# Attention followed by a gated product: one buffer for both banks of a block product's accumulator, a third held back, and new due times

## The chip, the cores and the metric

One core of one Trainium2 chip runs the whole program. The metric is device time in microseconds; the kernel before took 578.11 us (median of 3 runs, 578.06 to 578.78).

The names of the engines in the profile: PE is TensorE (matmuls; PEld are its weight loads), DVE is VectorE, ACT is ScalarE, POOL is GpSimd, SP is SyncE, which only issues DMAs here.

## The reference

```python
def _attn_ref(q, k, v):                     # q, k, v: 8 batches x 12 heads x 448 x 64
    S = q.shape[2]
    scores = scale * np.matmul(q, k.transpose(0, 1, 3, 2)) - np.log(S)
    attn = 1.0 / (1.0 + np.exp(-scores))    # a sigmoid, no row sums
    return np.matmul(attn, v)

def _moe_ref(x, w_val, conv_w, w_out):      # x: 8 x 448 x 768, the heads side by side
    for k in range(5):                      # causal convolution of 5 taps, each channel alone
        gate_pre += conv_w[k] * xp[:, k:k + S, :]
    gate = 1.0 / (1.0 + np.exp(-gate_pre))
    val = x @ w_val                         # 768 x 768
    return gate * val @ w_out               # 768 x 768
```

## The kernel before

**Layout and stages.** Channels lie on the 128 partitions, tokens run along the free dimension. Attention works on 48 pairs of heads (i) that go by twos (j, 24 of them; three j make a batch). The work of one j on PE is a chain: `scores_rest` of the next j, `attend` of this j, then `scores` of the next pair (L547, L570, L633, L641). ACT takes the sigmoid and splits the result into a high and a low 16-bit part, DVE takes the low part. Batch 0 is not multiplied on its own: each of the other seven batches carries a seventh of it, so that a product has 512 columns (448 + 64) and batches run from 1 to 7.

For a batch b there follow: the scale of x (`x_largest`, PE at L733), the split of x into two 16-bit parts (`x_split`), the gate (taps on ACT and DVE, some added up by DMAs that POOL issues, L714), the first product "val" (`product`, 6 columns m of 18 matmuls of 512 tokens, L965), the multiplication of its result by the gate on DVE (L975), and the second product "out".

**The block product.** For batches 6 and 7 the second product isn't six columns but `product_mixed`: a 2 x 2 block scheme with seven block products instead of eight. `form` makes from the gated result the seven input blocks (three in a first part of the tiles `form`/`form_hi`, `form_lo`, four in a second part, after sums on DVE at L844), `mix` has made the mixed weights once. The product is done by thirds q (NQ = 3, two column blocks each). A third has seven steps k; a step is nine matmuls of 256 columns (L904; three groups of three, one per c) into one of two banks, and then one evacuation of that bank into `y` with a scale: on ACT or DVE for steps 0, 1, 2 and 6 (L915, which shows as L386 on ACT or L388 on DVE), on DVE alone for steps 3, 4 and 5, which add to `y` (L917). The banks of the seven steps are 0, 1, 0, 1, 0, 1, 0. Steps 0, 3 and 5 use weights of `w_out`, the others the tile `mixed`. Batch 6 writes its results from `y`, batch 7, the last one ("final"), from `y_mixed`.

**Accumulators.** A third's two banks are one tile from the ring `ps_a` (L340: three buffers of two banks each). The same ring serves attention's scores and outputs and, for batch 7, the scale of x at L733. A ring hands out its buffers in the order of the program text, and a buffer's first writer may not be ordered ahead of the first writer of the buffer before it. So the three thirds of batch 6 come after L733 of batch 7, and the three final thirds replace those of batch 6, one by one. The val columns use two other banks (`ps_m0`, `ps_m1`) in turn.

**What sets the order.** The program text only makes a list of operations (`Plan.op`), each with the engines it may run on and their estimated costs, a due time (`prio`), and dependencies that follow from the `Buf` objects it reads and writes. `Plan.issue` (L196) then plays a list scheduler: whenever an engine is free it takes, among the operations that are ready by the estimates, the one with the smallest due time. The resulting order is the order of instructions on each engine. The semaphores between engines are not made from the `Buf` objects, but afterwards from the tiles that the instructions touch. `Buf.part` (L119) makes a second `Buf` for the same tile; operations on the part and on the whole are then independent for the scheduler.

Due times come from `line(i)` (L396: `first` for each of the first 12 pairs, `step` for each later one), `tau(i)` = line(i) + t_i, `turn(b)` = line(6(b + 1)) + b_b, and constants of the table `AT` (L85) for each kind of operation. A val column m is due at turn(b) + product + val_b + m step / 2; step k of third q of batch 6's block product at turn(6) + product + out6 + 3 step + mixed_mid + (q + k / 7) step; of the final one at turn(7) + product + out7 + 3 step + mixed + (3k + q) step / 21. HELD (L64) is how many of the three thirds of batch 6's product are put behind val of batch 7 in the program text (L1103 and L1109); these also get `AT["held"]` added to their due times.

Of the kernel before, what the change touches and what calls it, by code (L numbers as in the profile page):

```python
# [60 lines left out]
OUT_TOP = 13  # L61
HT = T // 2
NQ = NC // 2
HELD = 2  # L64
FORMS = 6
MIXED_FROM = 6
MIX_AT = 13
# [15 lines left out]


AT = dict(  # L85
    first=-23.17, step=19.9, val=118.94, val_step=-180.69, out=170.01, out_step=-585.1, w_max=-224.22,
    w_split=49, load_qk_first=12.5, load_qk=-153.59, load_v=35.43, split_hi=192.57, split_lo=97.07,
    rest_first=-5.45, rest=250.79, a_first=-823.33, a=-1541.85, attend=-104.6, v_max=-108.74, v_exp=-145.56,
    v_split=417.62, x=-65.05, x_max=32.83, x_scale=-888.7, x_hi=232.99, x_lo=156.41, x_step=393.39, tap=-573.02,
    scores=173.83, a_rest=-160.23, a_rest_first=-66.81, tap_first=75.93, tap_pair=-94.59, tap_step=190.04,  # L90
    gate=38.36, product=-249.46, y=72.69, g_hi=-142.47, g_lo=154.31, o=172.23, share=0.47, w_load=-45.48,
    mix=831.29, mix_step=13.64, form=7.6, mixed=12.32, t0=170.5, t1=-311.68, t2=-210.97, t3=24.02, t4=-165.77,
    t5=182.87, t6=37.77, t7=210.54, t8=130.07, t9=-208.47, t10=-178.97, t11=21.32, t12=26.04, t13=159.94,
    t14=143.46, t15=-16.02, t16=-1206.94, t17=269.84, t18=35.94, t19=51.33, t20=-168.57, t21=-153.86,
    t22=-150.38, t23=54.53, t24=-9.1, t25=-119.78, t26=128.3, t27=-16.04, t28=-248.21, t29=-216.39, t30=-23.16,
    t31=-188.65, t32=-25.47, t33=201.84, t34=-112.66, t35=116.16, t36=68.12, t37=132.66, t38=-271.95,
    t39=-148.99, t40=-170.95, t41=-163.89, t42=-172.96, t43=148.71, t44=-73.9, t45=-55.24, t46=-128.06,
    t47=205.12, t48=162.48, t49=-179.83, b0=-52.12, b1=184.23, b2=26.45, b3=-121.12, b4=-98.53, b5=-102.96,
    b6=239.3, b7=117.68, val0=-168.38, val1=-927.67, val2=243.52, val3=-124.5, val4=-183.24, val5=-32.09,
    val6=172.16, val7=-67.59, out0=13.17, out1=32.57, out2=-15.69, out3=-147.76, out4=351.75, out5=161.64,  # L100
    out6=125.89, out7=211.13, form_mid=-11.03, mixed_mid=-129.61, held=-17.53, o_mid=14.69,
)


# [169 lines left out]
def attention_then_gate(  # L274
# [32 lines left out]
    def ring(pool, n, shape, dtype, name):  # L307
        rings.append(Ring(pool, n, shape, dtype, name))
        return rings[-1]
# [8 lines left out]
    v_exp = ring(sb, 3, [P, 4], I32, "v_exp")  # L318
# [14 lines left out]
    x_max = ring(sb, 2, [P, NP], F32, "x_max")  # L333
# [13 lines left out]
    def fixed(shape, dtype, name):  # L347
        t = const.tile(shape, dtype, name=name)
        return Buf(lambda: t)
# [16 lines left out]
    def columns_of(t):  # L366
        return [Buf(t) for _ in range(NC)]
# [3 lines left out]
    w_max = {n: columns_of(fixed([P, NC], BF16, f"{n}_max")) for n in ("val", "out")}  # L371
# [6 lines left out]
    def copy(eng, to, x):  # L378
        if eng == "A":
            nc.scalar.copy(to, x)  # L380
        else:
            nc.vector.tensor_copy(to, x)  # L382
# [7 lines left out]
    def sub(eng, to, x, y):  # L390
        engines[eng].tensor_tensor(to, x, y, op=ALU.subtract)  # L391


    FIRST, STEP = AT["first"], AT["step"]

    def line(i):  # L396
        return min(i, AHEAD) * FIRST + max(i - AHEAD, 0) * STEP
# [4 lines left out]
    def turn(b):  # L402
        return line((b + 1) * NP) + AT[f"b{b}"]
# [368 lines left out]
    mixed = {}  # L772
# [75 lines left out]
    def product_mixed(b, only=range(NQ), late=0.0):  # L848

        final = b == B - 1  # L850
        t = turn(b) + AT["product"] + AT[f"out{b}"] + NC * STEP / 2 + AT["mixed" if final else "mixed_mid"] + late
# [11 lines left out]
        acc, ys, whole_y = {}, {}, {}  # L863

        def begin(q):
            if final:
                x = ps_a.new()
                acc[q] = [(x.part() if n else x, lambda n=n: x()[:, n, :HT]) for n in range(2)]
                y = x_ring.new(lambda: sb.tile([P, 2, T], F32, name="y_mixed", tag="x", bufs=x_ring.n))
                whole_y[q] = y  # L870
                ys[q] = [([y.part(), y.part() if n else y], lambda n=n: y()[:, n, :]) for n in range(2)]
            else:
                if b < IN_A_FROM:
                    x = next(bank)
                    xs = [x.new(), banks[x is banks[0]].new()]
                    acc[q] = [(x, lambda x=x: x()[:, :HT]) for x in xs]
                else:
                    x = ps_a.new()
                    acc[q] = [(x.part() if n else x, lambda n=n: x()[:, n, :HT]) for n in range(2)]
                ys[q] = {}  # L880

        def slot(q, n):
# [53 lines left out]
        if final:  # L936
            for q in range(NQ):
                begin(q)
            for k in range(len(steps)):
                for q in range(NQ):  # L940
                    step(k, q, t + (3 * k + q) * STEP / 21)
        else:
            for q in only:
                begin(q)
                for k in range(len(steps)):
                    step(k, q, t + (q + k / 7) * STEP)

    gv = {}

    def product(n, b, m, late=0.0):  # L950
        t = turn(b) + AT["product"] + AT[f"{n}{b}"] + (m + NC * (n == "out")) * STEP / 2 + late
        h, l = w_hi[n, m], w_lo[n, m]

        def columns(cs, t):
            po = next(bank).new()
            for c in range(NC):
                s = two[3 * b + c // 2]
                if n == "val":
                    x, reads = (lambda k, xs=s["xs"], p=c % 2: xs()[:, k, p * T : (p + 1) * T]), s["xs_in"]
                else:  # L960
                    x, reads = (lambda k, g=gv[b, c]: g()[:, k, :]), [gv[b, c]]

                def emit(e, c=c, x=x):
                    for j, (w, k) in enumerate(((h, 0), (h, 1), (l, 0))):
                        mm(po()[:, cs], w()[:, c, :], x(k)[:, cs], start=(c == 0 and j == 0),  # L965
                           stop=(c == NC - 1 and j == 2))

                op({"P": 0.65 * (cs.stop - cs.start) / T}, t + c * STEP / 12, emit, [*reads, h, l], [po])
            return po

        po = columns(slice(0, T), t)
        t += STEP / 2
        if n == "val" and b >= MIXED_FROM:
            g = st[b * NP + m]["g"]
            op({"V": 0.66}, t + AT["y"], lambda e: nc.vector.scalar_tensor_tensor(  # L975
                g()[:, m % 2, :], po(), y_scale()[:, m : m + 1], g()[:, m % 2, :], op0=ALU.mult, op1=ALU.mult), [po, y_scale], [g], port="")
            if m % 2:
                form(b, m // 2)
            return
        y = y_ring.new()  # L980
        if n == "val":
            g, gate = form_ring.new(lambda: sb.tile([P, 2, T], F16, name="g", tag="form", bufs=FORMS)), st[b * NP + m]["g"]
            gv[b, m] = g

            op({"V": 0.66}, t + AT["y"], lambda e: nc.vector.scalar_tensor_tensor(
                y(), po(), y_scale()[:, m : m + 1], gate()[:, m % 2, :], op0=ALU.mult, op1=ALU.mult), [po, gate, y_scale], [y], port="")
            op({"V": 0.33, "A": 0.53}, t + AT["g_hi"], lambda e: copy(e, g()[:, 0, :], y()), [y], [g])
            op({"G": 1.17, "V": 0.6}, t + AT["g_lo"], lambda e: sub(e, g()[:, 1, :], y(), g()[:, 0, :]), [y], [g])
        else:
            n = (b - 1) * SL  # L990
            op({"A": 0.65, "V": 0.66}, t + AT["o"], lambda e: scaled(
                e, y(), po(), outer[b]()[:, m : m + 1]), [po, outer[b]], [y], port="")
            op({"S": 0.45}, t + 1, lambda e: nc.sync.dma_start(out[b, m], y()[:, :S]), [y], [], P * S * 4)
            op({"S": 0.45}, t + 1.1, lambda e: nc.sync.dma_start(out[0, m, :, n : n + SL], y()[:, S:]), [y], [], P * 1000)
# [52 lines left out]
    for j in range(TWOS):  # L1047
# [7 lines left out]
        if j == 0:  # L1055
            first, attended = attend(j)
            last = attended.then = rest(j + 1)
        else:
            o = rest(j + 1) if j + 1 < TWOS else None
            first, last = attend(j)  # L1060
            if o:
                o.then = first
                o.deps |= {d for d in first.deps if d is not o}
                first = o
# [19 lines left out]
        b = j // 3  # L1084
# [15 lines left out]
        if b > 1:  # L1100
            x_unscale(b)
            if b - 1 >= MIXED_FROM:
                product_mixed(b - 1, range(NQ - HELD) if b == B - 1 else range(NQ))  # L1103
            else:
                for m in range(NC):
                    product("out", b - 1, m)
        for m in range(NC):
            product("val", b, m)
    product_mixed(B - 2, range(NQ - HELD, NQ), AT["held"])  # L1109
    product_mixed(B - 1)  # L1110
    plan.close(rings)
    for o in plan.issue():
# [50 lines left out]
```

## Time and profile before

| | |
|---|---|
| median of 3 runs | 578.11 us (578.06 to 578.78) |
| the profiled execution's own time | 578.0 us |
| span of the profile, first to last instruction | 576.2 us |
| granted TensorE clock | 1.000 |
| PE busy | 566.0 us, 98% of the span |
| DVE busy | 453.5 us, 79% |
| ACT busy | 448.5 us, 78% |
| POOL busy | 155.2 us, 27% |

In a line of the timeline the first two numbers are the start and the length in us, followed by engine, line and operation, what is written and read, and in brackets the idle time before it with what ended it. In the chain of waits each line is a start, a length and the work, "x18" being 18 instructions. In a table by stage each engine has its busy time and, in brackets, its instructions. Matmuls overlap: one of 256 columns is listed with 0.27 us, but the next one starts well before its end.

### The profile page before, as it was taken

How to read it: one execution, taken by the hardware profiler on the slowest of the kernel's cores; microseconds unless marked ns; L12 is line 12 of the kernel's file. 1: busy time of each engine (PE TensorE's matmuls, PEld its weight loads, DVE VectorE, ACT ScalarE, POOL GpSimd, SP SyncE). 2: the span in 40 equal slices, each digit the busy share in tenths (PEclk: the TensorE clock that was granted, in tenths of full speed). 3: DMA queues.
4: the chain of work that ended last, by engine and by line, in shares of the span. 5: the costliest groups of instructions: out<-in, count | busy, mean ns of one | idle time of the engine just before them, and what ended most of it. 6: DMA issues, size and time to landing. Idle time of an engine off the chain costs nothing.

```text
span 576.2 us, 9839 instructions
## 1 busy us (share of the span) xinstructions
PE 566.0 (98%) x3742; PEld 294.1 (51%) x3742; DVE 453.5 (79%) x742; ACT 448.5 (78%) x612; POOL 155.2 (27%) x177
## 2 busy tenths in 40 slices
PE   9999989999999999999999999999999999999897
PEld 5333334455555555545555454554545555545776
DVE  1778999998898988878587886879777889987312
ACT  5777998889998879878798878889688899852231
POOL 0000124344425332252322423223241433110100
PEclk9999999999999999999999999999999999999999
DMA  8798687757584475834667364674636653441213
GB/s 338 283 350 267 182 258 145 191 132 180 129 199 102 115 169 142 214 75 134 127 189 189 77 163 96 171 167 140 169 69 174 157 133 75 95 89 38 73 38 111
DMA packets 39935, 88.45 MB, mean 154 GB/s; under 512 B 14928, under 2 KB 21072, under 8 KB 39888
## 3 DMA queue, kind: packets, MB, share of 16 engines
q0 software_dynamic: 8640, 31.46, 29.5%
q1 hardware_dynamic: 31248, 56.37, 29.4%
q8 instruction: 29, 0.48, 0.3%
q14 instruction: 18, 0.15, 0.1%
HBM read 43.96 MB, written 12.40 MB: 98 GB/s over the span
## 4 chain that ended last, share of the span: by engine, by line
PE 94%; ACT 4%; DVE 1%; issue 1%; ACTq 0%
PE ps_m L965 49%; PE ps_a L547 16%; PE ps_a L641 15%; PE ps_a L904 6%; PE ps_a L570 4%; PE ps_a L633 3%; ACT a_single L583 2%; PE ps_m L1008 1%; DVE y L917 1%; ACT y_mixed L386 0%; ACT tap L386 0%; ACT w_words L386 0%; DVE gate L844 0%; ACT y L386 0%; ACT x L380 0%
## 5 line engine op out<-in xcount | busy, mean ns | idle before, releaser
L965 PE MATMUL ps_m<-xs,w_val_hi 128*128 128x512 f16 x504 | 150.1, 379 | 0.0
L391 POOL TENSOR_TENSOR qk_lo<-qk_src,qk_hi 128x448 fp32r<-128x448 f32 x66 | 79.3, 1222 | 138.4 <-DVE qk_hi L382 80.6
L594 DVE SCALAR_TENSOR_TENSOR a<-ps_a,a 128x896 f16<-128x896 f32 x96 | 101.5, 1085 | 11.7 <-ACT a L386 11.3
L965 PE MATMUL ps_m<-g,w_out_hi 128*128 128x512 f16 x360 | 107.2, 379 | 0.0
L583 ACT ACTIVATE ps_a<-ps_a 128x896 f32<-128x896 f32 x112 | 99.4, 910 | 8.5 <-DVE v_exp L575 6.8
L965 PE MATMUL ps_m<-xs,w_val_lo 128*128 128x512 f16 x252 | 95.5, 379 | 0.0
L386 ACT ACTIVATE tap<-x,cw 128x512 f32<-128x512 f32 x120 | 85.9, 739 | 1.4 <-issue 1.4
L714 POOL DMA_DIRECT2D gate<-tap x60 | 52.9, 882 | 121.2 <-DMA gate<-tap 25.9
L386 ACT ACTIVATE a<-ps_a 128x896 f16<-128x896 f32 x96 | 85.2, 928 | 0.0
L965 PEld LDWEIGHTS <-w_val_hi 128*128 128x128 f16 x504 | 47.7, 98 | 59.5 <-issue 6.5
L965 PE MATMUL ps_m<-g,w_out_lo 128*128 128x512 f16 x180 | 68.2, 379 | 0.0
L965 PEld LDWEIGHTS <-w_out_hi 128*128 128x128 f16 x360 | 34.0, 98 | 43.5 <-issue 4.6
L641 PE MATMUL ps_a<-a,v_hi 128*64 128x448 f16 x384 | 52.7, 354 | 0.0
L583 ACT ACTIVATE a_single<-ps_a 128x896 f32<-128x896 f32 x56 | 47.7, 929 | 5.0 <-PE ps_a L547 3.3
L965 PEld LDWEIGHTS <-w_val_lo 128*128 128x128 f16 x252 | 24.7, 98 | 29.7
L547 PE MATMUL ps_a<-qk_hi 64*128 64x448 f32 x198 | 39.7, 398 | 0.0
L641 PE MATMUL ps_a<-a_single,v_src 128*64 128x448 f32 x192 | 37.8, 543 | 0.0
L547 PE MATMUL ps_a<-qk_single 64*128 64x448 f32 x180 | 37.2, 551 | 0.0
L547 PE MATMUL ps_a<-qk_lo,qk_hi 64*128 64x448 f32 x198 | 36.2, 362 | 0.0
L710 DVE SCALAR_TENSOR_TENSOR gate<-x,cw,gate 128x512 f32<-128x512 f32 x48 | 36.1, 754 | 0.1
L547 PE MATMUL ps_a<-qk_hi,qk_lo 64*128 64x448 f32 x198 | 36.1, 362 | 0.0
L386 ACT ACTIVATE x<-ps_a,v_exp 128x896 f32<-128x896 f32 x16 | 16.2, 1010 | 24.7 <-PE ps_a L641 24.7
(154 smaller groups left out, 898.0 us busy)
## 6 DMA issues: line engine op xcount, KB each, us to landing
gate<-tap POOLq DMA_DIRECT2D x60, 512.0 KB, 4.9
qk_src<-qk SPq DMA_DIRECT2D x33, 448.0 KB, 4.8
v_src<-vs SPq DMA_DIRECT2D x24, 448.0 KB, 4.9
out_t<-y SPq DMA_DIRECT2D x36, 224.0 KB, 3.3
qk_single<-qk SPq DMA_DIRECT2D x15, 448.0 KB, 6.0
w_words<-w_val SPq DMA_DIRECT2D x6, 768.0 KB, 8.7
w_words<-w_out SPq DMA_DIRECT2D x6, 768.0 KB, 6.0
x<-first_x SPq DMA_DIRECT2D x21, 68.0 KB, 4.4
```

The costliest lines, as they stand in the source:

```text
L386: nc.scalar.activation(to, x, AF.Copy, scale=by)
L391: engines[eng].tensor_tensor(to, x, y, op=ALU.subtract)
L547: mm(b()[:, h, :S], k()[rows, at : at + P], q()[rows, :S], start=(n == 0), stop=(n == len(terms(i)) - 1))
L570: mm(b()[to, h, :S], x[n]()[rows, CW:], x[n]()[rows, :S], start=True, stop=True)
L583: nc.scalar.activation(to, b()[:, :, :S], AF.Sigmoid, bias=-math.log(S), scale=1.0 / math.sqrt(D))
L594: op({"V": 1.0}, t + 0.5, lambda e: nc.vector.scalar_tensor_tensor(part(1), p(), A_SCALE, part(0), op0=ALU.mult, op1=ALU.subtract), [b], [ ...
L633: mm(px()[to, p, :S], v()[rows, h * D : (h + 1) * D], x(s["a"])[rows, h, at : at + S], start=(j > 0 and n == 0), stop=(j == 0 and n == len ...
L641: mm(px()[to, p, :S], v()[:, o : o + D], x(st[2 * j + p]["a", c])[:, h, at : at + S], start=(j == 0 and c == 0 and n == 0), stop=(j > 0 an ...
L710: op({"V": 0.67}, at + AT["tap_step"] * k + AT["tap_pair"] * p, lambda e, p=p, part=part, k=k: nc.vector.scalar_tensor_tensor(part(), x()[ ...
L714: op({"G": 1.1}, at + AT["tap_step"] * k, lambda e, tap=tap: nc.gpsimd.dma_start(g(), tap(), accum_op=ALU.add), [tap], [g], 4 * P * T * 4, "")
L904: mm(to(), stat[a](), src()[:, f, :], start=(first and c == 0 and j == 0), stop=(c == NQ - 1 and j == 2), skip_group_check=True)
L965: mm(po()[:, cs], w()[:, c, :], x(k)[:, cs], start=(c == 0 and j == 0), stop=(c == NC - 1 and j == 2))
```

## The change

Five things are edited. In `product_mixed`, both banks of a third's accumulator become one `Buf`, for batch 6 and for the final product. HELD goes from 2 to 1, so two thirds of batch 6's product stand ahead of val of batch 7 in the text, and one behind. The steps of batch 6's product are spread over due times by STEP + mid_more instead of STEP. A val column m of batch 7 is due m val_more earlier or later. And every constant of `AT` has a new value; the table gains `val_more` and `mid_more`. No instruction is added or removed; the order on each engine changes.

```diff
-HELD = 2
+HELD = 1
...
 AT = dict(
-    first=-23.17, step=19.9, val=118.94, val_step=-180.69, out=170.01, out_step=-585.1, w_max=-224.22,
-    w_split=49, load_qk_first=12.5, load_qk=-153.59, load_v=35.43, split_hi=192.57, split_lo=97.07,
-    rest_first=-5.45, rest=250.79, a_first=-823.33, a=-1541.85, attend=-104.6, v_max=-108.74, v_exp=-145.56,
-    v_split=417.62, x=-65.05, x_max=32.83, x_scale=-888.7, x_hi=232.99, x_lo=156.41, x_step=393.39, tap=-573.02,
-    scores=173.83, a_rest=-160.23, a_rest_first=-66.81, tap_first=75.93, tap_pair=-94.59, tap_step=190.04,
-    gate=38.36, product=-249.46, y=72.69, g_hi=-142.47, g_lo=154.31, o=172.23, share=0.47, w_load=-45.48,
-    mix=831.29, mix_step=13.64, form=7.6, mixed=12.32, t0=170.5, t1=-311.68, t2=-210.97, t3=24.02, t4=-165.77,
...
-    t47=205.12, t48=162.48, t49=-179.83, b0=-52.12, b1=184.23, b2=26.45, b3=-121.12, b4=-98.53, b5=-102.96,
-    b6=239.3, b7=117.68, val0=-168.38, val1=-927.67, val2=243.52, val3=-124.5, val4=-183.24, val5=-32.09,
-    val6=172.16, val7=-67.59, out0=13.17, out1=32.57, out2=-15.69, out3=-147.76, out4=351.75, out5=161.64,
-    out6=125.89, out7=211.13, form_mid=-11.03, mixed_mid=-129.61, held=-17.53, o_mid=14.69,
+    first=-11.66, step=23.2, val=-115.92, val_step=-183.72, out=124.94, out_step=-470.51, w_max=73.34,
+    w_split=-219.2, load_qk_first=-161.37, load_qk=-68.86, load_v=-120.88, split_hi=407.94, split_lo=-8.28,
+    rest_first=142.49, rest=639.4, a_first=-1075.3, a=-1544.98, attend=-14.11, v_max=96.77, v_exp=-59.24,
+    v_split=312.9, x=118.14, x_max=-76.31, x_scale=-873.1, x_hi=75.99, x_lo=287.19, x_step=48.02, tap=-561.46,
+    scores=181.36, a_rest=-32.33, a_rest_first=158.34, tap_first=108.75, tap_pair=13.67, tap_step=208.61,
+    gate=129.4, product=-255.51, y=-86.31, g_hi=-192.09, g_lo=35.19, o=-165.84, share=0.61, w_load=12.03,
+    mix=558.71, mix_step=-100.8, form=-13.81, mixed=-6.22, t0=211.79, t1=54.82, t2=131.08, t3=206.23, t4=197.57,
...
+    t40=-173.08, t41=-18.14, t42=-152.85, t43=23.07, t44=-11.71, t45=-61.65, t46=-53.26, t47=16.55, t48=176.65,
+    t49=-9.27, b0=-104.34, b1=-187.38, b2=147.89, b3=138.94, b4=35.06, b5=-101.28, b6=246.12, b7=93.08,
+    val0=28.09, val1=-626.52, val2=-20.51, val3=164.64, val4=-144.63, val5=98.84, val6=179.85, val7=118.83,
+    out0=-193.47, out1=-207.48, out2=30.11, out3=169.39, out4=59.13, out5=-183.26, out6=124.68, out7=111.63,
+    val_more=-2.6, mid_more=160.73, form_mid=-164.89, mixed_mid=-324.71, held=-210.3, o_mid=190.85,
 )
...
             if final:
                 x = ps_a.new()
-                acc[q] = [(x.part() if n else x, lambda n=n: x()[:, n, :HT]) for n in range(2)]
+                acc[q] = [(x, lambda n=n: x()[:, n, :HT]) for n in range(2)]
...
                     x = ps_a.new()
-                    acc[q] = [(x.part() if n else x, lambda n=n: x()[:, n, :HT]) for n in range(2)]
+                    acc[q] = [(x, lambda n=n: x()[:, n, :HT]) for n in range(2)]
...
                 for k in range(len(steps)):
-                    step(k, q, t + (q + k / 7) * STEP)
+                    step(k, q, t + (q + k / 7) * (STEP + AT["mid_more"]))
...
         t = turn(b) + AT["product"] + AT[f"{n}{b}"] + (m + NC * (n == "out")) * STEP / 2 + late
+        if n == "val" and b > MIXED_FROM:
+            t = t + m * AT["val_more"]
```

More of the change, by code (lines that the diff above doesn't have):

```diff
@@ L91 @@
-    gate=38.36, product=-249.46, y=72.69, g_hi=-142.47, g_lo=154.31, o=172.23, share=0.47, w_load=-45.48,
-    mix=831.29, mix_step=13.64, form=7.6, mixed=12.32, t0=170.5, t1=-311.68, t2=-210.97, t3=24.02, t4=-165.77,
-    t5=182.87, t6=37.77, t7=210.54, t8=130.07, t9=-208.47, t10=-178.97, t11=21.32, t12=26.04, t13=159.94,
-    t14=143.46, t15=-16.02, t16=-1206.94, t17=269.84, t18=35.94, t19=51.33, t20=-168.57, t21=-153.86,
-    t22=-150.38, t23=54.53, t24=-9.1, t25=-119.78, t26=128.3, t27=-16.04, t28=-248.21, t29=-216.39, t30=-23.16,
@@ L96 @@
-    t31=-188.65, t32=-25.47, t33=201.84, t34=-112.66, t35=116.16, t36=68.12, t37=132.66, t38=-271.95,
-    t39=-148.99, t40=-170.95, t41=-163.89, t42=-172.96, t43=148.71, t44=-73.9, t45=-55.24, t46=-128.06,
-    t47=205.12, t48=162.48, t49=-179.83, b0=-52.12, b1=184.23, b2=26.45, b3=-121.12, b4=-98.53, b5=-102.96,
-    b6=239.3, b7=117.68, val0=-168.38, val1=-927.67, val2=243.52, val3=-124.5, val4=-183.24, val5=-32.09,
-    val6=172.16, val7=-67.59, out0=13.17, out1=32.57, out2=-15.69, out3=-147.76, out4=351.75, out5=161.64,
@@ new lines @@
+    scores=181.36, a_rest=-32.33, a_rest_first=158.34, tap_first=108.75, tap_pair=13.67, tap_step=208.61,
+    gate=129.4, product=-255.51, y=-86.31, g_hi=-192.09, g_lo=35.19, o=-165.84, share=0.61, w_load=12.03,
+    mix=558.71, mix_step=-100.8, form=-13.81, mixed=-6.22, t0=211.79, t1=54.82, t2=131.08, t3=206.23, t4=197.57,
+    t5=-122.73, t6=175.99, t7=126.89, t8=-95.04, t9=-216.09, t10=-609.76, t11=76.72, t12=-206.96, t13=-164.74,
+    t14=-75.58, t15=-62.65, t16=-1479.52, t17=47.57, t18=83.1, t19=93.37, t20=-171.31, t21=-117.13, t22=89.07,
@@ new lines @@
+    t23=130.99, t24=-206.74, t25=-290.54, t26=-201.22, t27=161.06, t28=-110.92, t29=-43.09, t30=-69.04,
+    t31=86.81, t32=107.77, t33=-192.91, t34=286.9, t35=72.86, t36=157.37, t37=-185.75, t38=86.9, t39=4.65,
+    t40=-173.08, t41=-18.14, t42=-152.85, t43=23.07, t44=-11.71, t45=-61.65, t46=-53.26, t47=16.55, t48=176.65,
+    t49=-9.27, b0=-104.34, b1=-187.38, b2=147.89, b3=138.94, b4=35.06, b5=-101.28, b6=246.12, b7=93.08,
+    val0=28.09, val1=-626.52, val2=-20.51, val3=164.64, val4=-144.63, val5=98.84, val6=179.85, val7=118.83,
```

## The prediction

> **What bounds the kernel now.** I read the page's busy shares first, then the busy time by stage, then what PE waited for, then the chain of waits and the timeline around those waits.
>
> ```profile
> span 576.2 us, 9839 instructions
> ...
> PE 566.0 (98%) x3742; PEld 294.1 (51%) x3742; DVE 453.5 (79%) x742; ACT 448.5 (78%) x612; POOL 155.2 (27%) x177
> ```
>
> PE is the bound, and the edit leaves every matmul in place, so only the time in which PE isn't fed can change. By stage (span, then PE, PEld, DVE, ACT, POOL busy, granted clock, DMA share, GB/s):
>
> ```profile
> 30.00:90.00 60.00, 57.46 (x334) 21.86 (x333) 55.81 (x102) 52.00 (x68) 8.19 (x11) 1.00 0.85 260
> 90.00:300.00 210.00, 210.00 (x1374) 107.47 (x1372) 184.18 (x301) 181.84 (x252) 78.59 (x83) 1.00 0.62 147
> 300.00:460.00 160.00, 160.00 (x1071) 81.76 (x1071) 126.87 (x198) 133.73 (x182) 49.13 (x55) 1.00 0.59 144
> 460.00:500.00 40.00, 40.00 (x294) 21.05 (x291) 35.75 (x55) 36.50 (x48) 12.74 (x12) 1.00 0.48 105
> ...
> 532.50:563.60 31.10, 28.18 (x241) 23.39 (x240) 8.29 (x17) 8.91 (x19) 2.12 (x1) 1.00 0.16 52
> ```
>
> From 90 to 500 us PE has no idle time: a new order can win nothing there, only lose. The open places are 30 to 90 (60.00 - 57.46 = 2.5 us) and 532.5 to 563.6, the block products of the last two batches. A busy matmul hides its pitch, so I take the pitch from the chain of waits, and the loss from the weight loader, which stalls as long as PE isn't fed:
>
> ```profile
> 563.63 9.02 PE ps_a L904 x81
> ```
> ```profile
> its engine sat idle before it (us, times) until:
>   issue: 4.9, 11
> ```
> ```profile
> PE ps_a L904 <- DVE y L917: 1.7, 6, 0.4
> PE ps_a L733 <- ACT diagonal L386: 1.5, 1, 1.5
> PE ps_m L1008 <- DVE ones L1001: 1.1, 1, 1.1
> PE ps_a L570 <- ACT a_single L583: 1.0, 3, 0.6
> PE ps_a L904 <- ACT y_mixed L386: 1.0, 4, 0.3
> PE ps_a L904 <- ACT y L386: 0.2, 1, 0.2
> ```
>
> 81 matmuls of 256 columns in 9.02 us, the last lasting 0.27, is (9.02 - 0.27) / 80 = 0.109 us each. The 241 in the 31.10 us stage need 26.3 us, so 4.8 are lost; the loader says 4.9, in 11 stops (for line 904, the block products). All of PE's waits are in the last fence: 6 + 4 + 1 of line 904 behind DVE and ACT, the rest at the start, none behind a DMA. One stop in the timeline:
>
> ```profile
> 545.71 0.27 PE L904 MATMUL ps_a<-form_hi,w_out_lo 128*128 128x256 f16 x1
> ...
> 546.02 0.47 ACT L386 ACTIVATE y_mixed<-ps_a,o_scale 128x256 f32<-128x256 f32 x1 [1.17 <-PE ps_a L904]
> 546.03 0.27 PE L904 MATMUL ps_a<-form_hi,w_out_lo 128*128 128x256 f16 x1
> ...
> 546.54 0.27 PE L904 MATMUL ps_a<-form_hi,mixed 128*128 128x256 f16 x1 [0.23 <-ACT y_mixed L386]
> ```
>
> This is the first y_mixed evacuation of all. It empties step 0 of the final product's first third (weights w_out, bank 0). By the due times in the code, what waits for it is step 1 of that third: weights "mixed", bank 1. So a matmul into bank 1 waits until bank 0 is evacuated: on the chip the two banks already act as one buffer, while the scheduler before orders work as if they were two. Step 0's last matmul starts at 545.71, step 1 goes on at 546.54: 0.83 us, of which 0.109 is pitch; 0.72 must be filled with other work. A neighbour's whole step (9 x 0.109 = 0.98 us) fills it. The last 81 matmuls, where three thirds take turns step by step, show that: no stop.
>
> The Trainium skill ("PSUM — Partial Sum Buffer", section on bank collisions) says that accesses of two engines to different banks run clean, and to guard PSUM by bank. By that rule the single buffer would serialise what may overlap, the separate banks would be right, and the gain would be nil (578.0, in the second rival). The row at 546.54 disagrees about this program: its waits are by the whole tile.
>
> **The change part by part.** The profiled execution took 578.0 us, 1.8 more than its span and 0.1 less than the median of the runs, 578.11; I sum against 578.0.
>
> *One buffer for both banks.* No instruction goes. A step becomes ready, for the scheduler, only after the other bank's evacuation, so it puts another third's step or val columns (three 512-column matmuls) into the 0.72 us. This can remove up to 4.9 us; if the order still puts two steps of one third side by side, each stop stays at 4.9 / 11 = 0.45.
>
> *One third held, mid_more, val_more, the new due times.* I worked the due times out of both lists; after, say, pair-line 42 is 12 x -11.66 + 30 x 23.2 = 556.1, batch 6's turn 556.1 + 246.1 = 802.2, and its product's first step 802.2 - 255.5 + 124.7 + 3 x 23.2 - 324.7 = 416.3; step k of third q comes (q + k/7) x (23.2 + 160.7) later, the held third 210.3 earlier again. Before, all 21 steps of batch 6's product are due at 365 to 404, after the last val columns (239 to 297): they only plug holes there and pile up behind, as the chain shows:
>
> ```profile
> 497.15 3.99 PE ps_m L965 x18
> 501.15 0.06 PE ps_a L733 x2
> 501.20 3.93 PE ps_a L904 x36
> 505.13 7.77 PE ps_m L965 x36
> 512.90 0.33 PE ps_a L904 x3
> 513.23 3.88 PE ps_m L965 x18
> ```
>
> After, the first third is due at 416 to 574, ahead of val (652 to 706); the second at 600, 627, 653, 679, 705, 732, 758; the held one at 574, 600, 626, 653, 679, 705, 732. So six steps fall among the val columns, which cover an evacuation, and three come behind (732, 758, 732). Each moved step carries 9 matmuls and one evacuation, each third four output DMAs. The evacuations (0.47 us on ACT here, 0.48 on DVE) go into 505 to 532.5, and the DMAs leave earlier on SP, whose last ones, of the final product, set the end as before:
>
> ```profile
> 505.00:532.50 27.50, 27.50 (x140) 13.48 (x138) 21.34 (x34) 10.71 (x15) 2.58 (x3) 1.00 0.32 61
> ```
> ```profile
> 551.57 0.48 DVE L917 SCALAR_TENSOR_TENSOR y<-ps_a,o_scale,y 128x256 f32<-128x256 f32 x1 [9.08 <-ACT y L386]
> ...
> 571.92 1.58 SPq L930 DMA_DIRECT2D out_t<-y_mixed  x3
> ```
>
> ACT has 16.8 us free there and DVE 6.2, for at most some 18 evacuations, 8.6 us over both: hidden. Without that cover each is a stop of 0.45.
>
> What is late next is batch 7's last form. From the last val matmul to its second part:
>
> ```profile
> 532.30 0.38 PE L965 MATMUL ps_m<-xs,w_val_lo 128*128 128x512 f16 x1
> ...
> 539.75 2.12 POOL L391 TENSOR_TENSOR form_lo<-gate,form_hi 128x1024 f16<-128x1024 f32 x1 [19.16 <-ACT form_hi L380]
> ```
>
> 539.75 + 2.12 - 532.30 = 9.6 us; between them lie the column's evacuation, the first part of the form (ready early enough for a step 0), its sums and the cast. Before, held work covered all of it. After, three held steps (2.9), the final product's three first steps (2.9, needing only the form's first part) and two thirds of its second steps (2.0) give 7.8: from none to 1.8 us short; nearer none if the low part goes to DVE instead of POOL. I take 0.8.
>
> So the tail: -4.9, +0.4 (one stop left), +0.8 = -3.7; bounds -4.9 and 0.
>
> *The gap after the last attention.* From 497.15 to the x scale at 501.15 (L733), PE's only cover is val columns of batch 6 (18 matmuls, 3.99 us); block products can't start before L733 because of the order of the three ps_a buffers. Before, val 6 is due at 481 to 531 and the last attend at 496; after, val 6 at 727 to 785 and attend at 858, so by due time nothing would be left over. But columns also wait for banks, and the profile is full of columns that were due first and yet let attention pass after two:
>
> ```profile
> 339.80 7.88 PE ps_m L965 x36
> 347.67 2.02 PE ps_a L547 x18
> 349.69 7.88 PE ps_m L965 x36
> ```
>
> Bounds 0 and +4.0; I take 0, the value of this trace, and price the rest as a rival.
>
> *The other due times* (loads, splits, taps, gates, y, o). From 90 to 500 ACT and DVE keep 352 and 346.8 us busy of 410, so reordering has 58 and 63 us of cover: 0. No PE wait is on a DMA, POOL or SP, so the moved loads and gate DMAs cost 0 while that holds. The start's waits (the longest, 1.5, behind "ACT diagonal") may go or double, -2.5 to +2.5; I take 0: DVE is busy 55.81 of 60 there, ACT 52.00, so neither sign is favoured.
>
> Sum: 578.0 - 3.7 = **574.3 us**, 0.7% below the median.
>
> **The rivals.**
> (a) The start's waits go as well: 574.3 - 2.5 = 571.8. For it: only 2.5 us are to be found. Against: three engines are nearly full there.
> (b) No change. The gap after the last attention loses its cover: 574.3 + 4.0 = 578.3; or the change doesn't do what it says: the new order keeps steps side by side, or the two banks are in truth independent and forcing their steps apart buys nothing, so the stops stay: 578.0. For it: val 6 is due ahead of the last attend. Against: the pairs of columns above.
> (c) Slower. Attention's chain (rest, attend, scores) moves from due 218 to 536 to due 848 to 1297, behind all products. If a pair of columns (7.88 us) passes a chain piece in 460 to 500, ACT, busy 36.50 of 40, has 3.5 to make it up, so attention ends 4.4 later, val 6 is used up, and the 4.0 gap opens too: 574.3 + 8.4 = 582.7. It decides once such idle time exceeds the 3.7 gained. For it: ACT's 91% there. Against: products are due ahead of the chain in most batches now, and PE has no idle time from 90 to 500.
>
> **How the numbers follow.** This kernel can tell 0.2% (1.2 us) from no change. Forecast (572.3 to 576.8): 0.61; (a) 0.13; (b) 0.13; (c) 0.13. Faster is the forecast and (a), 0.74; same (b), 0.13; slower (c), 0.13. The range reaches down past (a) to 571.0 (all of 4.9 and 2.2 gained) and up to 579.0 past (b), leaving (c) out.
>
> **What would show it.** Right: in the last 75 us "PE ps_a L904" waits fall from 11 to a few, single three-matmul groups among val columns become whole steps, and less than 31 us lies between the last val matmul and the long run of L904. The buffer step is wrong if waits of 0.2 to 0.4 us behind y evacuations remain; the cover steps if a PE idle of 1 us or more stands before L733, before the first form_hi matmul, or in attention (L641, L633) behind ACT. A loss between 90 and 460 would make the whole forecast wrong.

## The result and the profile after

The kernel after takes 574.35 us (median of 6 runs, 573.59 to 575.12). In the same comparison the kernel before takes 578.49 us (6 runs, 578.06 to 579.21). The ratio is 0.9927 with a 95% interval of 0.9915 to 0.9940: 0.7% faster, by more than the 0.2% that can be told. The forecast was 574.3 us.

The profiled execution took 573.81 us. The page begins with its span and the busy shares:

```profile
span 572.0 us, 9843 instructions
...
PE 565.1 (99%) x3742; PEld 294.1 (51%) x3742; DVE 449.0 (78%) x714; ACT 459.7 (80%) x633; POOL 167.7 (29%) x184
```

The span is 4.2 us shorter with the same 3742 matmuls. The engines' own instructions are 9015 in both (the five counts of the row), but the scheduler also moved work between engines: DVE has 28 fewer, ACT 21 and POOL 7 more. The four more in the total are semaphore instructions. All of PE's waits in the kernel after:

```profile
PE ps_a L733 <- ACT diagonal L386: 1.5, 1, 1.5
PE ps_m L1010 <- DVE ones L1003: 1.1, 1, 1.1
PE ps_a L570 <- ACT a_single L583: 0.3, 1, 0.3
PE ps_m L967 <- DVE xs L768: 0.2, 1, 0.2
```

The three rows of line 904 (six, four and one wait) are gone and nothing of that line has come back. Of the three waits behind `a_single` at the start one is left. New is the last row, a val column that waits for the split of x. The stages, with the same columns as before:

```profile
30.00:90.00 60.00, 58.20 (x336) 22.06 (x335) 53.98 (x101) 52.85 (x70) 10.36 (x12) 1.00 0.82 250
90.00:300.00 210.00, 209.88 (x1371) 107.24 (x1369) 184.37 (x284) 186.67 (x263) 84.38 (x88) 1.00 0.61 147
300.00:460.00 160.00, 160.00 (x1071) 81.75 (x1071) 128.10 (x191) 136.33 (x188) 52.37 (x57) 1.00 0.59 145
460.00:500.00 40.00, 40.00 (x293) 21.01 (x290) 34.31 (x54) 36.71 (x49) 12.41 (x11) 1.00 0.45 98
500.00:530.00 30.00, 29.72 (x193) 18.58 (x192) 21.00 (x36) 16.09 (x24) 3.44 (x4) 1.00 0.44 87
530.00:563.00 33.00, 33.00 (x264) 25.66 (x263) 13.01 (x24) 10.06 (x18) 3.76 (x2) 1.00 0.14 45
```

The middle is as full as it was, and the last stage, where 28.18 of 31.10 us were busy by the old order, is now full too. The chain of waits shows the new order of the last 80 us:

```profile
497.27 4.64 PE ps_m L967 x21
501.91 0.07 PE ps_a L733 x2
...
518.83 1.97 PE ps_a L904 x18
520.79 0.65 PE ps_m L967 x3
521.77 0.65 PE ps_m L967 x3
...
541.27 0.65 PE ps_m L967 x3
541.91 26.54 PE ps_a L904 x243
568.46 0.02 issue
```

Block products now stand among the val columns up to 541.91, and from there 243 matmuls run at (26.54 - 0.27) / 242 = 0.109 us without one stop. Of the 243, 189 are the final product; the other 54, as many as six steps have, are the end of batch 6's product. Before, 132 matmuls of batch 6 came behind the last val matmul.

The last attention ends at the same time in both: the last matmul of its last attend starts at 496.80 before (by the timeline) and 496.92 after. So all of the 4.2 us lies behind it. There the stops of line 904 (4.9 us) are gone, and two gaps are new at the first val columns of batch 7. The timeline shows that the first waits for the split of x, and the chain of waits that the second follows the emptying of a val bank by DVE (line 977):

```profile
505.64 0.38 PE L967 MATMUL ps_m<-xs,w_val_hi 128*128 128x512 f16 x1 [0.19 <-DVE xs L768]
```
```profile
506.25 0.67 DVE gate L977
506.97 2.75 PE ps_m L967 x12
```

By the starts of the matmuls they cost 0.36 and 0.25 us. The sum is -4.9 + 0.6 + 0.1 = -4.2 us.

### The profile page after: what moved, and what is told of

It is laid out like the page before. It is cut to its first block, busy times and chain, and to the rows that moved or that the text cites. A ratio compares the mean times of both kernels' runs of the same rounds, so it can differ in the third digit from the quotient of the medians.

```text
span 572.0 us, 9843 instructions
## 1 busy us (share of the span) xinstructions
PE 565.1 (99%) x3742; PEld 294.1 (51%) x3742; DVE 449.0 (78%) x714; ACT 459.7 (80%) x633; POOL 167.7 (29%) x184
## 4 chain that ended last, share of the span: by engine, by line
PE 89%; ACT 5%; DVE 4%; issue 1%; POOL 0%; DVEq 0%; ACTq 0%
PE ps_m L967 46%; PE ps_a L547 15%; PE ps_a L641 14%; PE ps_a L904 7%; PE ps_a L570 3%; PE ps_a L633 2%; DVE gate L710 1%; ACT a L386 1%; ACT tap L386 1%; ACT ps_a L583 1%; ACT a_single L583 1%; PE ps_m L1010 1%; DVE w_words L414 1%; DVE x_max L689 0%; DVE out_max L440 0%
## 5 line engine op out<-in xcount | busy, mean ns | idle before, releaser
L714 POOL DMA_DIRECT2D gate<-tap x60 | 56.0, 934 | 181.0 <-ACT tap L386 64.9
```

Of the source, the lines that this page charges most:

```text
L714: op({"G": 1.1}, at + AT["tap_step"] * k, lambda e, tap=tap: nc.gpsimd.dma_start(g(), tap(), accum_op=ALU.add), [tap], [g], 4 * P * T * 4, "")
```

## The experiments

The theory at the start, A: the two banks of one accumulator tile work as one buffer on the chip, so keeping their steps apart removes the stops, and the new due times serve only to have other work at hand for it. The rival, B: the due times alone do it, and the single buffer is worth nothing. Each kernel was timed in five rounds beside the kernel before; ratios are to it.

### The parts back in the kernel after

```diff
-                acc[q] = [(x, lambda n=n: x()[:, n, :HT]) for n in range(2)]
+                acc[q] = [(x.part() if n else x, lambda n=n: x()[:, n, :HT]) for n in range(2)]
```

(at both places)

> The kernel after, with the second bank as a part of its own for the scheduler again (both places); due times, HELD, mid_more and val_more stay new. Theory A (the chip waits by the whole tile, and the single buffer is what lets the scheduler see it): stops of PE behind y and y_mixed evacuations come back at line 904, 3 to 8 of the 11, each 0.45 us: 575.7 to 578.0 us. Rival B (the new due times alone keep the steps apart): no stop comes back, 574.4 +- 0.6 us.

Measured: 576.49 us (575.93 to 577.12), ratio 0.9966 [0.9954, 0.9979]. Some waits of line 904 are back, all behind evacuations into `y`, two on DVE and two on ACT, and none behind `y_mixed`; the second fence is of the stalls of its weight loader (us in total, times), which also counts shorter ones:

```profile
PE ps_a L904 <- DVE y L917: 0.7, 2, 0.4
PE ps_a L904 <- ACT y L386: 0.5, 2, 0.3
```
```profile
  issue: 2.6, 7
```

So the single buffer is worth about 2.1 us with the rest of the change in place (576.49 against 574.35), and the loader's 2.6 us are about that size. A held; B, by which the time would have stayed, fell.

### The single buffer alone

The same two lines, the other way round, in the kernel before.

> The kernel before with the single buffer alone; HELD 2 and the old due times. Theory A (the edit only corrects what the scheduler believes; the due times have to use it): the 11 stops at line 904 fall to 3 or fewer, but before the first val column of batch 7 only three first steps can start (18 matmuls, 2.0 us, where 36 stood), and the pile behind val is still one third after the other, so PE stands idle for the form or the evacuations instead: 576.5 to 580 us. Rival C (the buffer is all of the gain): 574.3 us. Rival B (the due times are all of it): 578.5 +- 0.6, stops as before.

Measured: 580.29 us (579.29 to 580.78), ratio 1.0028 [1.0017, 1.0039]: slower than before, just outside of what A expected, and with nine waits of line 904 where at most three were expected. Its waits, and the end of its chain:

```profile
PE ps_a L904 <- DVE y_mixed L917: 1.8, 3, 0.6
PE ps_a L904 <- ACT y_mixed L386: 1.7, 3, 0.6
...
PE ps_a L904 <- DVE y L917: 0.5, 2, 0.3
PE ps_a L904 <- ACT y L386: 0.4, 1, 0.4
```
```profile
539.01 25.02 PE ps_a L904 x225
...
564.58 1.16 PE ps_a L904 x9
566.28 1.16 PE ps_a L904 x9
567.99 1.16 PE ps_a L904 x9
569.78 1.16 PE ps_a L904 x9
...
573.22 1.16 PE ps_a L904 x9
```

The loader of line 904 stalls 5.9 us in nine stops here, where it stalled 4.9 us in eleven. The chain shows what took the gain. Single steps of nine matmuls follow one another every 1.70 to 1.79 us. A step needs 9 x 0.109 = 0.98, so each loses 0.72 to 0.81: the round trip of the prediction, no longer filled. With the old due times the scheduler left 150 matmuls of batch 6 behind val and let them and two final thirds run on together. The last third then was alone, and a third alone has nothing to put between its steps. These six steps use the two banks of their tile in turn, so each waited for the emptying of the bank that it doesn't write. Keeping steps apart does no good by itself: another third has to be there until the end.

### Two tiles of its own for one third

This one tests the disputed point by itself, in the kernel before. The two banks of the first final third become two separate tiles, those of the val columns, which are free by then. The due times stay.

```diff
-                x = ps_a.new()
-                acc[q] = [(x.part() if n else x, lambda n=n: x()[:, n, :HT]) for n in range(2)]
+                if q == 0:
+                    acc[q] = [(x, lambda x=x: x()[:, :HT]) for x in (banks[0].new(), banks[1].new())]
+                else:
+                    x = ps_a.new()
+                    acc[q] = [(x.part() if n else x, lambda n=n: x()[:, n, :HT]) for n in range(2)]
```

> The kernel before, but the first third of the final product accumulates in two tiles of their own (the two banks that val has done with), not in the two banks of one tile. Nothing else changes. Theory A (a matmul into one bank waits for the other bank's evacuation because both are one tile): the stops that this third's steps met (at 546.5 before, and up to two more behind y_mixed) go, 11 stops become 8 to 10, the time 577.2 to 578.1. Rival E (the waits are not by the tile, but by the bank or the engines' order): 11 stops, 578.5 +- 0.5, the stop at 546.5 still there.

Measured: 577.21 us (11 runs, 576.55 to 578.14), ratio 0.9977 [0.9968, 0.9986]. Lines stand three lower here, so line 904 is 907:

```profile
PE ps_a L907 <- DVE y L920: 1.7, 6, 0.4
...
PE ps_a L907 <- ACT y L386: 0.2, 1, 0.2
```

All four waits behind `y_mixed` are gone, one more than was expected at most, and the seven of batch 6, whose banks are still in one tile, have stayed. But the order of the final product's matmuls changed as well, so that other groups now stand between the steps of this third, and the count alone proves little. Single rows prove more:

```profile
547.46 0.47 ACT L386 ACTIVATE y_mixed<-ps_m,o_scale 128x256 f32<-128x256 f32 x1 [1.17 <-PE ps_m L907]
...
547.81 0.27 PE L907 MATMUL ps_a<-form_hi,w_out_lo 128*128 128x256 f16 x1
...
547.91 0.27 PE L907 MATMUL ps_m<-form_hi,mixed 128*128 128x256 f16 x1
```

The matmul at 547.91 writes bank 1 and comes on the pitch, while bank 0 is being emptied until 547.93. The same happens at 559.78 (until 559.80) and 565.89 (until 565.92). In the kernel before, the matmul at 546.54 came 0.05 us after the evacuation at 546.02 had ended. So in the traces PE waits by the whole tile, as the six single steps of the experiment before show, and not where the banks are tiles of their own. That part of A is shown, though the overlap seen between the steps is only 0.02 to 0.03 us long. Separate tiles are also another way to the same end: the change only teaches the scheduler that two banks of one tile don't overlap.

### The new constants alone

The new values of the constants that the kernel before has too; two banks as parts, HELD = 2, and the two new constants at zero.

```diff
-HELD = 1
+HELD = 2
...
-    val_more=-2.6, mid_more=160.73, form_mid=-164.89, mixed_mid=-324.71, held=-210.3, o_mid=190.85,
+    val_more=0.0, mid_more=0.0, form_mid=-164.89, mixed_mid=-324.71, held=-210.3, o_mid=190.85,
...
+                acc[q] = [(x.part() if n else x, lambda n=n: x()[:, n, :HT]) for n in range(2)]
```

> The kernel before with nothing but the new values of the due times that it already had: separate parts for the banks, HELD 2, no mid_more, no val_more. Theory A (due times can't avoid a wait that the scheduler doesn't know of): four or more stops of 0.4 us at line 904 behind y and y_mixed evacuations, none or few steps left behind val: 576 to 579 us. Rival B (the due times are the gain): 574.4 +- 0.6 us.

Measured: 581.68 us (581.47 to 581.93), ratio 1.0045 [1.0033, 1.0057], slower than either theory had it; B fell clearly. Its waits name what neither theory had named:

```profile
PE ps_a L904 <- ACT form_hi L380: 1.8, 1, 1.8
...
PE ps_a L904 <- DVE y L917: 1.0, 3, 0.4
PE ps_a L904 <- DVE form_lo L391: 0.7, 1, 0.7
```

With these constants no step of batch 6 is left behind the last val matmul (553.53), and PE waits bare for batch 7's last form, 1.76 and 0.72 us. That is the shortage which the prediction had priced at 0.8. The four stops behind evacuations into `y` are there, as A expected. The time is 2.7 us over its range; the wait for the form (2.5) and a fall of the clock after it (last section) are enough for that.

### The new constants with the single buffer

As in the last experiment, but with two banks as one buffer.

> The fourth corner of the square {separate banks, one buffer} x {HELD 2 without mid_more and val_more, HELD 1 with both}, all with the new due times: one buffer, HELD 2, mid_more and val_more 0. The other three gave a ratio to before of 1.0045 (separate, off), 0.9966 (separate, on) and 0.9927 (one, on). Theory A (buffer and reserve act on different losses, stops and the wait for the last form): one buffer takes the 0.4 us stops away but not the wait for the form: 1.9 us and more before the first final step stay; 577.5 to 580.5 us. Rival G (the two act on the same loss, and either does): 574.4 to 576.

Measured: 576.31 us (575.76 to 576.84), ratio 0.9962 [0.9951, 0.9974]. That is better than A expected by more than 1 us: a miss. The form is waited for less than A had it, and one longer stop is left:

```profile
PE ps_a L904 <- DVE y L917: 0.9, 1, 0.9
PE ps_a L904 <- DVE form_lo L391: 0.6, 2, 0.4
```

Here 21 matmuls of batch 6 are left behind val, none without the single buffer. So the single buffer has a second effect, on the reserve for the form: it seems that steps kept apart stretch batch 6's product in the schedule. What it shows with the earlier runs, as ratios:

| all with the new constants | banks as parts | one buffer |
|---|---|---|
| HELD = 2, mid_more and val_more 0 | 1.0045 | 0.9962 |
| HELD = 1, mid_more 160.73, val_more -2.6 | 0.9966 | 0.9927 |

The buffer is worth 0.83% alone, the three settings 0.79% alone, both together 1.18% and not 1.62%. The traces say the same: from the last matmul of attention to the end of the span it is 82.55 and 77.09 us in the upper row, 77.46 and 75.11 in the lower, so the buffer is worth 5.45 us without the settings and 2.35 with them. They are two remedies for partly the same loss. Of the 3.1 us between the two, about 1.4 are the fall of the clock that the profile of the upper left kernel shows.

### The three settings one by one

In the kernel after, each in a kernel of its own:

```diff
-    val_more=-2.6, mid_more=160.73, form_mid=-164.89, mixed_mid=-324.71, held=-210.3, o_mid=190.85,
+    val_more=-2.6, mid_more=0.0, form_mid=-164.89, mixed_mid=-324.71, held=-210.3, o_mid=190.85,
```

> The kernel after with mid_more 0: all three thirds of batch 6's product are then due ahead of val of batch 7. Theory A (the spread keeps steps in reserve among and behind the val columns): little is left to cover batch 7's last form, PE idles 1 to 4 us at the first final steps, or meets stops in the bunched steps: 575.3 to 578.4 us. Rival F (the spread is of no account once the buffer is right): 574.4 +- 0.6 us.

```diff
-HELD = 1
+HELD = 2
```

> The kernel after with HELD 2: the second third is then also due 210 earlier (390 to 548 instead of 600 to 758), ahead of val of batch 7. Theory A (what counts is how many steps are left for the time behind val's last matmul, where batch 7's last form needs 9 us): instead of 54 matmuls of batch 6 some 20 to 30 are left, PE waits 0.5 to 2 us for a form or an evacuation: 574.8 to 576.6 us. Rival F (reserve is of no account once the buffer is right): 574.4 +- 0.6 us.

```diff
-    val_more=-2.6, mid_more=160.73, form_mid=-164.89, mixed_mid=-324.71, held=-210.3, o_mid=190.85,
+    val_more=0.0, mid_more=160.73, form_mid=-164.89, mixed_mid=-324.71, held=-210.3, o_mid=190.85,
```

> The kernel after with val_more 0: the later val columns of batch 7 are due up to 13 later, so up to half a step's spacing more of the block steps goes ahead of them. Theory A: fewer steps left behind val, 0 to 1.5 us of waits for the last form or an evacuation: 574.4 to 576.0 us. Rival F: 574.4 +- 0.6 us.

The interval of HELD = 2 lay over that of the kernel after, so it was run again, beside the unchanged kernel after:

> The kernel after, unchanged, as the measure for the others of this call: ratio to before 0.9915 to 0.994.

> The kernel after with HELD 2 once more, beside the kernel after on one chip. Theory A: 0.5 to 2 us slower than after, with a wait for a form or an evacuation to be seen in the trace. Rival F: within 0.5 us of it.

| kernel | us (runs) | ratio [95%] | matmuls of batch 6 behind val | us from attention's last matmul to the end |
|---|---|---|---|---|
| after | 574.35 (573.59 to 575.12) | 0.9927 [0.9915, 0.9940] | 54 | 75.11 |
| after again | 574.86 (573.62 to 575.00) | 0.9931 [0.9919, 0.9943] | 54 | 75.11 |
| mid_more = 0 | 575.43 (574.40 to 575.83) | 0.9943 [0.9929, 0.9956] | 24 | 75.94 |
| HELD = 2 | 575.12 (574.93 to 575.88) | 0.9935 [0.9923, 0.9947] | 27 | 76.45 |
| HELD = 2 again | 575.84 (575.05 to 576.32) | 0.9954 [0.9941, 0.9966] | 27 | 76.46 |
| val_more = 0 | 576.13 (575.68 to 577.10) | 0.9950 [0.9938, 0.9963] | 45 | 77.16 |

By the ratios each setting is worth some 0.1 to 0.2% (0.5 to 1.3 us), but the intervals touch or nearly touch those of the kernel after, so the times alone don't settle it. The last column does. It is from one profile each and leaves out the start, which differs between executions of one kernel (last section); two profiles of the same kernel agree in it within 0.01 us. By it the settings are worth 0.83, 1.34 and 2.05 us, and F falls for each. The waits say why, with one row each; the first is of mid_more = 0, then HELD = 2 again (HELD = 2 has the same row), then val_more = 0:

```profile
PE ps_a L904 <- DVE form_lo L391: 0.5, 1, 0.5
```
```profile
PE ps_a L904 <- DVE form_lo L391: 1.0, 2, 0.7
```
```profile
PE ps_a L904 <- DVE y_mixed L917: 1.2, 2, 0.6
```

Without one of the first two, too little of batch 6 is left (24 and 27 matmuls, 2.6 and 2.9 us) and the form shows, for less than the 1 to 4 us that A had for mid_more. Without the third, 45 are left and no form is waited for, which is not what A expected: the first final step starts at 534.95, before the last val matmul at 543.52; the last third ends alone, and the round trip is open twice (0.85 us from matmul to matmul, as in the single buffer alone). So it isn't only how many steps are kept: the kernel after has enough of them behind val and its final thirds end in turn, and neither loss touches it.

### Other due times

The last kernel keeps the change but takes the constants of the table from a search at random, of neighbouring values, for the earliest end by the scheduler's own estimate (1.2 us earlier than for the kernel after).

```diff
-    first=-11.66, step=23.2, val=-115.92, val_step=-183.72, out=124.94, out_step=-470.51, w_max=73.34,
+    first=-6.18, step=22.8, val=-402.26, val_step=-159.5, out=17.97, out_step=-712.09, w_max=1024.62,
...
-    val_more=-2.6, mid_more=160.73, form_mid=-164.89, mixed_mid=-324.71, held=-210.3, o_mid=190.85,
+    val_more=3.32, mid_more=170.88, form_mid=-263.35, mixed_mid=-327.5, held=-227.83, o_mid=42.11,
```

> The kernel after with other due times, found by changing them at random and keeping what ends earlier by the scheduler's own estimate. Theory A (with one buffer the estimate is true to the chip within some 0.3 us a place): the wait at the start before L733 falls from 1.5 to about 0.7 us, the one of 0.6 us in the first val column of batch 7 to 0.3, no stop at line 904: 0.8 to 1.4 us faster than the kernel after, 573 to 573.8. Rival H (what is left is below what the estimate gets right): within 0.6 us of after.

Measured: 575.82 us (574.63 to 578.07), ratio 0.9955 [0.9940, 0.9970]. The waits of line 904 are none here too, the one for the split of x is gone, and the longest one of the start is halved. But others stand in its place:

```profile
PE ps_a L547 <- ACT x L380: 0.7, 1, 0.7
PE ps_a L733 <- ACT diagonal L386: 0.7, 1, 0.7
PE ps_a L547 <- DVE a_rest L594: 0.5, 1, 0.5
```

The estimate's 1.2 us weren't there on the chip, and the kernel is 1.0 us slower than the kernel after beside it, more than H allowed. The stretch behind attention did get shorter, 74.62 us against 75.11, but attention's last matmul starts 1.5 us later than in the kernel after, counted from the first matmuls of line 570. No kernel of the study is faster than the kernel after.

## Why the prediction was right

**The buffer step (-4.9, of which 0.4 stays).** The direction and the cause hold. The experiments with the single buffer and with separate tiles show that the waits are by the whole tile. All eleven stops went, so the term is -4.9, and the 0.4 set aside for a last stop is not there. But the step was told as the buffer's own work, and that was wrong: alone it costs time (1.0028), since its stops move to a third that ends alone. It was asked whether two steps of one third would stand side by side, and not which third would have company at the end. The rival "the change doesn't do what it says" fell with the first experiment. The Trainium skill ("Perfetto Trace Analysis", section "Matmuls") says to rotate independent groups of matmuls through different PSUM banks, so that one's evacuation overlaps the next one's matmuls. The kernel before did rotate within a tile, yet did not overlap: each of its eleven stops cost 0.45 us on average, and 0.73 to 0.81 where nothing stood between the steps (single buffer alone). With the banks in two tiles matmuls came before the evacuation had ended, so the rule holds here between tiles and not within one.

**The late form (+0.8).** Mis-sized: it is 0. The order has six steps of batch 6 behind val and not three (54 matmuls in all, 5.9 us and not 2.9). Also, the second part of the form came sooner, as these rows of the timeline show:

```profile
541.53 0.38 PE L967 MATMUL ps_m<-xs,w_val_lo 128*128 128x512 f16 x1
...
548.86 1.23 DVE L391 TENSOR_TENSOR form_lo<-gate,form_hi 128x1024 f16<-128x1024 f32 x1 [0.20 <-ACT form_hi L380]
```

548.86 + 1.23 - 541.53 = 8.6 us, not 9.6: the low part ran on DVE in 1.23 us, where it took POOL 2.12 before (the prediction's "if the low part goes to DVE"). The cover of 5.9 + 2.9 + 2.0 = 10.8 us exceeds it by 2.2. That the shortage is real, the neighbouring kernels show: waits for the form of 1.8 + 0.7 with no matmul left, 0.6 with 21, 0.5 with 24, 1.0 with 27, and none with 33, 45 and 54. The count is not all that decides, since the kernel with 27 waits longer than the one with 24.

**The gap after the last attention (0).** Right: 21 matmuls of val, three more than before, stand between the last attend and L733. With that goes rival (c): from 300 to 500 PE has no idle time, though `scores_rest`, the head of each chain, is due behind all products. The 848 to 1297 of the prediction are its due times alone; by the constants of `AT` the attends and scores of the same pairs are due at 322 to 870.

**Other due times (0).** Right from 90 to 500 (0.12 us of 410). At the start two of the three waits behind `a_single` went and the stage of 30 to 90 gained 0.7 us, but the last matmul of attention starts 0.1 us later than before, so the rest of the way took it back; rival (a) did not happen. Not foreseen was the 0.6 at batch 7's first val columns. Three val matmuls more stand ahead of L733, so the scale of x comes 0.8 later (501.91 against 501.15), and less stands between it and batch 7's first column. By the timeline that is 18 matmuls of block products and 6 of val (18 x 0.109 + 6 x 0.216 = 3.3 us), where there were 36 and 9 (5.9 us); the split of x needs more than the 3.3. That is the first gap, 0.36; the other 0.25 is the wait for the val bank that DVE emptied at 506.25.

The sum was -3.7, and measured -4.2: 0.4 and 0.8 too dear, 0.6 + 0.1 left out. That 574.3 lies so near 574.35 is partly luck, as the kernel before was also 0.4 us slower in this comparison than the 578.11 from which the forecast came.

**The signs.** The waits of line 904 fell (to none), and 0.4 us, less than 31, lies between the last val matmul and the long run. The third sign was wrong: single groups of three between val columns did not become whole steps. Some did (three runs of 18 and one of nine stand there), but there were seven such groups, and there are now 15, as the chain's val groups 0.98 us apart show (0.65 and three block matmuls). They cost nothing, since a val column stands on either side.

**What stays open.** Why a column of val shifted by 2.6 in its due time sends the final thirds ahead; that was seen in one order of the schedule and not traced back. Also why the form is waited for longer with 27 matmuls left than with 24.

## What to carry to other kernels

A scheduler that thinks two halves of a tile independent orders work into a wait that the chip then makes; either tell it so or give the halves tiles of their own, and measure the round trip (here 0.72 us beyond a matmul's pitch) to know how much other work each step needs beside it. At the end of a kernel that round trip and the latency of the last input want the same thing, a reserve of independent steps: count what is left when the last input's work starts, and whether the last parts end in turn. And an edit that sets such an order free is judged with its due times, not alone: here the buffer alone lost 0.3%, the constants alone 0.45%, and all together won 0.7%.

## What was not expected of the hardware

**The clock fell after two short stops.** In the kernel with the new constants alone PE had 1.76 and 0.72 us of idle time (by the timeline) within 553.5 to 557, with one matmul between. The stages behind them, with the granted clock third from the end:

```profile
553.50:557.40 3.90, 1.42 (x10) 0.86 (x9) 2.43 (x4) 1.16 (x2) 0.00 (x0) 1.00 0.00 0
557.40:561.00 3.60, 3.60 (x20) 2.44 (x19) 2.20 (x4) 1.93 (x4) 0.00 (x0) 0.53 0.00 0
561.00:575.00 14.00, 14.00 (x123) 11.80 (x122) 3.99 (x9) 2.77 (x7) 0.00 (x0) 1.00 0.21 67
```

For 3.6 us the clock was 0.53, and 20 matmuls ran in the time of 33: 13 x 0.109 = 1.4 us more, so in this execution the two stops and the fall behind them took some 4 us and not 2.5. The 1.4 us are about half of what this kernel was slower than the upper end of what was expected (579). The Trainium skill ("TensorE: Matmul & The Clock Gate", section "Why this matters for your kernels") warns of idle gaps of more than about 3 us; here neither was that long. No run separates the fall from the stops, and the times don't bear it out: four of this kernel's five runs show a mean clock of 0.996, but the one with 1.000 is the slowest (581.93). In the kernel with the single buffer alone it is the other way round: its three runs with 0.998 are the slowest (580.43 to 580.78, the other four 579.29 to 580.29).

**The first matmuls differ between executions.** Two profiles of the same kernel after, at their first 24 matmuls:

```profile
4.41 4.78 PE L547 MATMUL ps_a<-qk_single 64*128 64x448 f32 x24
```
```profile
4.40 6.10 PE L547 MATMUL ps_a<-qk_single 64*128 64x448 f32 x24
```

The second takes 1.3 us longer for them, and the whole span is 1.2 us longer (573.2 against 572.0), though the order of the 3742 matmuls is the same. The granted clock is shown as 1.00 over 4.40 to 10.50 in both, so the rows don't say why. The difference is about the spread of this kernel's runs (573.6 to 575.1), and as large as what the single settings are worth.
